# Rounding a float64 weight's high part before its low word is added, in a pooled attention and gated MLP kernel

## The chip, the cores and the metric

The kernel runs on one core of a Trainium2 chip. Its time is the device time of one launch in microseconds; times are medians over several runs. A profile records one further execution: its rows are in microseconds from the start of the span (first to last instruction). Engines are PE (TensorE, with PEld for its weight loads), DVE (VectorE), ACT (ScalarE), POOL (GpSimd) and SP, whose queue issues nearly all DMAs.

## The reference

For each of 8 batches, attention with 8 heads of 64 over 576 positions, with keys and values averaged over groups of 8 positions (72 pooled positions), then a gated MLP with a spatial gate:

```python
k_p = k.reshape(B, H, Sp, 8, D).mean(axis=3)          # v_p likewise
attn = softmax(scale * q @ k_p.T)                      # 576 x 72 per head
x = attn @ v_p                                         # (8, 576, 512)
h = gelu(x @ w_in)                                     # w_in (512, 1024)
u, v = h[..., :512], h[..., 512:]
v_n = (v - mean) / sqrt(var + 1e-6) * g_ln
v_s = einsum('ts,bsd->btd', w_sg, v_n) + b_sg
out = x + (u * v_s) @ w_out                            # w_out (512, 512)
```

`w_in` and `w_out` arrive as float64, all else as float32.

## The kernel before

All large products are made in three matmuls on numbers split in two: a value x is held as a high part, x rounded to the matmul's format (fp32r), and a low part, x minus the high part; high*high, high*low and low*high are accumulated. So each weight must become a pair of tiles: `wih`/`wil` for w_in, `woh`/`wol` for w_out.

**The float64 weights.** [...] The weights come in as six raw buffers of 1 MB (`load_w`: v0-1 and v2-3 for the v half of w_in, u0-1 and u2-3 for the u half, o0-1 and o2-3 for w_out), each holding two pieces of 128 x 512 numbers, low and high words alternating. `step_w` converts one of the twelve pieces in four steps:

1. ScalarE, L278: the high word is rescaled in exponent into a new tile `top` (tag y0 or y1).
2. DVE, L280: `top` is shifted left by 3. ScalarE, L281: the low word is turned, in its place, into the integer that its highest bits make.
3. POOL, L283: the two are added as integers into `top`, which now is the weight as float32. Then `move` (L221) rounds it into the high tile: on POOL (L223) for v0 to v3, u0, u3 and o2, on ScalarE (L225) for u1, u2, o0, o1 and o3.
4. `combine` (L227): `top` minus the high tile gives the low tile, on DVE for v3, u0, u2, o0 and o1, on POOL for the other seven.

**Buffers.** A tile takes a place in on-chip memory by its tag, and the next tile of that tag waits until every instruction that reads or writes the tile before it is done. The raw buffers borrow places that the batches need later: `load_w` gives v0-1 and v2-3 the tags `vhhi` and `vhlo`, u0-1 `ghi`, u2-3 `glo`, o0-1 `x32` (two places), and o2-3 `ghi` again, after u0-1. The gate of batch 0 (`ghi` for its high part, `glo` for its low part, made in `step_W`) takes the last two over.

**Order.** The order of all work is written out by hand (ORDER): each entry advances one step of one stage of one batch, and every engine issues its instructions in that order; semaphores are added by the framework. Stages are S (scores and softmax), T (attention turned round), V (attention times values), J and H (the v half), U (the u half), W (the spatial gate), O (the output product), Z (the store). Around o3, ORDER has: o3's third step, the first two steps of W0, W3 and W1, their third steps (the gate is rounded into `ghi`, on ScalarE in batch 0), o3's fourth step, then the fourth steps of W3 (on DVE, L228) and of W0 and W1 (on POOL, L228), then W2. The O stage reads `ghi` and `glo` by gate block d = 0, 1, 2, 3.

Of the kernel before, what the change touches and what calls it, by code (L numbers as in the profile page):

```python
# [8 lines left out]
F32 = mybir.dt.float32  # L9
# [5 lines left out]
ALU = mybir.AluOpType  # L15
# [79 lines left out]
def tile_pooled_attn_gmlp(ctx: ExitStack, tc: tile.TileContext, q, v0, vt0, k, v, vleft, w_in, w_sg, bg, w_out, out):  # L95
    nc = tc.nc
# [124 lines left out]
    def move(o, i, key):  # L221
        if key in OTHER:
            nc.gpsimd.tensor_copy(o, i)  # L223
        else:
            nc.scalar.copy(o, i)  # L225

    def combine(o, x, y, op, key):  # L227
        (nc.vector if key in OTHER else nc.gpsimd).tensor_tensor(o, x, y, op=op)  # L228
# [10 lines left out]
    def split(hi, lo, src, eng):  # L239
        nc.scalar.copy(hi, src)  # L240
        yield
        eng.tensor_tensor(lo, src, hi.bitcast(F32), op=ALU.subtract)
# [18 lines left out]
    def step_w(name, c):  # L261
        x = st["w", name, c // 2]
        n = x.shape[2] // 2
        x = x[:, c % 2:c % 2 + 1] if name == "v" else x[:, :, n * (c % 2):n * (c % 2 + 1)]
        hi, lo = {"v": (wih, wil), "u": (wih, wil), "o": (woh, wol)}[name]
        sl = (slice(None), slice(c, c + 1), slice(DF2, 2 * DF2)) if name == "v" else \
            (slice(None), slice(0, KC), slice(c * P, (c + 1) * P))
        hi, lo = hi[sl], lo[sl]
        if x.dtype == I32:

            rv = x.rearrange("p c (f w) -> p c f w", w=2)
            low, high = rv[:, :, :, 0], rv[:, :, :, 1]
            shape = [P, hi.shape[1], hi.shape[2]]
            top = per.tile(shape, I32, name="top", tag=f"y{c % 2}")
            nc.scalar.activation(top.bitcast(F32), high.bitcast(F32), AF.Prelu, scale=2.0 ** -112, alpha=2.0 ** 32)  # L278
            yield
            nc.vector.tensor_scalar(top, top, 3, None, op0=ALU.logical_shift_left)  # L280
            nc.scalar.activation(low, low.bitcast(U32), AF.Copy, scale=2.0 ** -29)  # L281
            yield
            nc.gpsimd.tensor_tensor(top, top, low, op=ALU.add)  # L283
            top = top.bitcast(F32)
            move(hi, top, f"{name}{c}h")
            yield
            combine(lo, top, hi.bitcast(F32), ALU.subtract, f"{name}{c}d")
            return
        yield from split(hi, lo, x, nc.gpsimd)

# [489 lines left out]
    def weight(name):  # L780
        if name[0] == "l":
            i = int(name[2])
            if name[1] == "s":
                load_wsg(i)
            else:
                load_w(name[1], i)
        else:
            if name not in going:
                going[name] = (step_s if name[0] == "s" else step_w)(name[0], int(name[1]))
            next(going[name], None)  # L790
# [70 lines left out]
```

## Time and profile before

| | |
|---|---|
| median of 3 runs | 498.75 us (498.43 to 500.1) |
| the profiled execution, own time | 500.95 us |
| its span | 499.2 us |
| PE busy | 492.0 us, 99% |
| DVE, ACT, POOL busy | 381.1, 271.4, 246.6 us |
| mean granted TensorE clock | 0.989 |

Busy time is counted by instruction; PE's overlaps its weight loads. In a timeline row, the first number is the start, the second the length, and the bracket at its end the idle time of that engine just before it, with what ended it. A row with "x2" merges two instructions that follow one another.

### The profile page before, as it was taken

What the parts mean: (1) busy time and instruction counts of PE and PEld (TensorE: products, weight loads), DVE (VectorE), ACT (ScalarE), POOL (GpSimd) and SP (SyncE); (2) the same over time, 40 slices, a digit from 0 to 9 for tenths busy, and PEclk for the clock granted to TensorE, in tenths of its full rate; (3) what the DMA queues carried; (4) which work ended last, traced back from release to release, by engine and by line L of the source; (5) the groups of instructions that cost most, each with busy time, mean ns of one, the idle gap of its engine ahead of it and who ended that gap; (6) DMA issues with size and microseconds to landing.
All of it is one profiled execution on the core that took longest, in us unless ns stands there. A gap on an engine that the chain in (4) does not pass through costs nothing.

```text
span 499.2 us, 9462 instructions
## 1 busy us (share of the span) xinstructions
PE 492.0 (99%) x3554; PEld 463.3 (93%) x3554; DVE 381.1 (76%) x593; ACT 271.4 (54%) x535; POOL 246.6 (49%) x330
## 2 busy tenths in 40 slices
PE   8989999999999999999999999999999999999997
PEld 8558999799899999999999999999999999999997
DVE  4967898677887887998889787978879757764462
ACT  4868984394747555658447364565735543314110
POOL 5875966544468357472484432845255720333010
PEclk9978999999999999999999999999999999999999
DMA  8992354666846352617434535143350333001003
GB/s 292 395 380 68 109 171 128 171 183 191 234 124 170 113 196 85 195 42 230 116 118 138 137 102 178 44 138 95 102 166 19 84 90 118 25 1 49 25 1 119
DMA packets 43034, 66.64 MB, mean 133 GB/s; under 512 B 5564, under 2 KB 22060, under 8 KB 42988
## 3 DMA queue, kind: packets, MB, share of 16 engines
q1 hardware_dynamic: 42700, 65.59, 43.5%
q8 instruction: 28, 0.46, 0.4%
q10 hardware_dynamic: 288, 0.44, 0.2%
q14 instruction: 18, 0.15, 0.1%
HBM read 47.14 MB, written 18.73 MB: 132 GB/s over the span
## 4 chain that ended last, share of the span: by engine, by line
PE 91%; DMA 4%; ACT 2%; DVE 2%; SPq 1%; issue 0%; ACTq 0%
PE mps L146 75%; PE aps L146 15%; DMA raw<-in_moe_w_in 3%; DMA out<-x 1%; PE aps L190 1%; SPq L237 1%; DVE ssum L466 0%; ACT e L457 0%; ACT x L219 0%; ACT L212 0%; ACT vg L480 0%; DVE x L755 0%; DVE x L217 0%; DVE ah L217 0%; DVE vl L424 0%
## 5 line engine op out<-in xcount | busy, mean ns | idle before, releaser
L146 PE MATMUL mps<-xhl,wih 128*128 128x288 f32 x512 | 84.2, 287 | 0.0
L146 PE MATMUL mps<-wih,xhl 128*128 128x512 f32 x256 | 79.4, 387 | 0.0
L146 PEld LDWEIGHTS mps<-xhl,wih 128*128 128x128 f32 x512 | 71.7, 189 | 0.3
L447 POOL TENSOR_TENSOR e<-e,ssum 128x720 f32<-128x720 f32 x29 | 41.9, 1444 | 60.3 <-DVE ssum L446 55.7
L146 PEld LDWEIGHTS mps<-wih,xhl 128*128 128x128 f32 x256 | 48.7, 191 | 6.8 <-DVE x L755 0.3
L146 PE MATMUL mps<-wsh,vhh 128*128 128x288 f32 x256 | 52.9, 288 | 0.0
L146 PE MATMUL mps<-wsh,vhl 128*128 128x288 f32 x256 | 52.3, 286 | 0.0
L146 PE MATMUL mps<-wsl,vhh 128*128 128x288 f32 x256 | 52.3, 286 | 0.0
L146 PE MATMUL mps<-xhl,wil 128*128 128x288 f32 x256 | 52.3, 286 | 0.0
L146 PE MATMUL mps<-ghi,woh 128*128 128x288 f32 x244 | 50.7, 288 | 0.0
L212 ACT ACT_TABLE_LOAD x39 | 50.0, 1283 | 0.6
L146 PE MATMUL mps<-ghi,wol 128*128 128x288 f32 x244 | 50.2, 286 | 0.0
L146 PE MATMUL mps<-glo,woh 128*128 128x288 f32 x244 | 50.2, 286 | 0.0
L470 POOL TENSOR_TENSOR rstd<-mv,eps 128x1 f32<-128x1 f32 (+1 forms) x40 | 11.8, 294 | 76.0 <-DVE mv L666 75.6
L146 PE MATMUL mps<-wil,xhl 128*128 128x512 f32 x128 | 47.2, 385 | 0.0
L234 POOL TENSOR_TENSOR xhl<-x,xhl 128x576 fp32r<-128x576 f32 x22 | 32.4, 1490 | 23.7 <-PE aps L146 12.0
L146 PE MATMUL aps<-kbd,qT 128*128 128x144 f32 x300 | 42.8, 293 | 0.0
L146 PEld LDWEIGHTS aps<-kbd,qT 128*128 128x128 f32 x300 | 40.2, 195 | 2.4 <-issue 0.9
L716 DVE SCALAR_TENSOR_TENSOR mps<-mps,both 128x576 f32<-128x576 f32 x32 | 26.1, 816 | 20.0 <-PE mps L146 20.0
L755 DVE TENSOR_TENSOR x<-mps,x 128x576 f32<-128x576 f32 x30 | 22.4, 750 | 24.4 <-PE mps L146 24.2
L146 PEld LDWEIGHTS mps<-wsh,vhh 128*128 128x128 f32 x256 | 40.0, 189 | 0.9 <-PE aps L146 0.4
L228 POOL TENSOR_TENSOR glo<-u,ghi 128x576 fp32r<-128x576 f32 x18 | 26.7, 1493 | 28.4 <-ACT ghi L219 18.1
(176 smaller groups left out, 1247.8 us busy)
## 6 DMA issues: line engine op xcount, KB each, us to landing
qT<-in_q SPq DMA_DIRECT2D x31, 288.0 KB, 4.2
out<-x SPq DMA_DIRECT2D x31, 288.0 KB, 2.6
kraw<-in_k SPq DMA_DIRECT2D x14, 576.0 KB, 4.5
vraw<-in_v SPq DMA_DIRECT2D x14, 512.0 KB, 5.0
al<-tfar SPq DMA_DIRECT2D x20, 288.0 KB, 3.4
tfar<-y SPq DMA_DIRECT2D x56, 80.0 KB, 1.9
raw<-in_moe_w_in SPq DMA_DIRECT2D x4, 1024.0 KB, 7.9
tfar<-y SPq DMA_DIRECT2D x56, 64.0 KB, 2.1
```

The costliest lines, as they stand in the source:

```text
L146: nc.tensor.matmul(o, lhsT, rhs, start=start, stop=stop)
L190: nc.tensor.transpose(ps[:rows, i * P:(i + 1) * P], src(i), ident if i < NT - 1 else swap)
L212: nc.scalar.activation(early, eps[:, 0:1], func)
L228: (nc.vector if key in OTHER else nc.gpsimd).tensor_tensor(o, x, y, op=op)
L234: nc.gpsimd.tensor_tensor(lo, x, hi, op=ALU.subtract)
L237: queue.dma_start(o, i)
L447: (nc.gpsimd if key in OTHER else nc.vector).tensor_tensor(e, e, rec.unsqueeze(3).broadcast_to([P, NT, 2, SP]), op=ALU.mult)
L470: nc.gpsimd.tensor_tensor(rstd, var, eps[:n, 1:2], op=ALU.add)
L716: nc.vector.scalar_tensor_tensor(vs, vs, gcol[:, d:d + 1], bbc.rearrange("p (a n) -> p a n", a=2), op0=ALU.mult, op1=ALU.add)
L755: nc.vector.tensor_tensor(x, seen(ps[:, :, 0:HALF]), x, op=ALU.add)
```

## The change

In the third step the rounding comes ahead of the addition and reads `top` as it is after the shift, without the low word's bits; it still goes to POOL or ScalarE by the same list. The sum is no longer written into `top` but over the low word in the raw buffer, at a step of two words, and the fourth step reads it there. The high part is so rounded from a number that lacks the low word; the low part is made from the full sum.

```diff
             yield
-            nc.gpsimd.tensor_tensor(top, top, low, op=ALU.add)
-            top = top.bitcast(F32)
-            move(hi, top, f"{name}{c}h")
-            yield
-            combine(lo, top, hi.bitcast(F32), ALU.subtract, f"{name}{c}d")
+            move(hi, top.bitcast(F32), f"{name}{c}h")
+            nc.gpsimd.tensor_tensor(low, top, low, op=ALU.add)
+            yield
+            combine(lo, low.bitcast(F32), hi.bitcast(F32), ALU.subtract, f"{name}{c}d")
             return
```

## Rows read from the trace of the kernel before

**Rows 1.** The page, engines: busy us, share of the span, instructions.
```profile
PE 492.0 (99%) x3554; PEld 463.3 (93%) x3554; DVE 381.1 (76%) x593; ACT 271.4 (54%) x535; POOL 246.6 (49%) x330
```

**Rows 2.** Waits of PE: us in total, times, longest.
```profile
PE aps L190 <- DVE xhl L232: 0.9, 1, 0.9
```

**Rows 3.** Windows: length, busy time of engines, granted clock, DMA share, GB/s.
```profile
30.00:45.00 15.00, 13.46 (x59) 10.16 (x58) 9.21 (x13) 9.35 (x33) 9.24 (x8) 0.66 0.71 240
80.00:85.00 5.00, 5.00 (x43) 5.00 (x42) 4.93 (x7) 0.67 (x1) 2.55 (x2) 1.00 0.73 185
```

**Rows 4.** Instructions of tile `top`: min/median/max ns, first and last start.
```profile
L283 POOL TENSOR_TENSOR top<-top,raw x12: 1286/1294/1628, 9.5 to 73.5; 128x512 int32<-128x512 int32 x12
...
L228 POOL TENSOR_TENSOR wol<-top,woh x2: 1286/1287/1288, 70.2 to 76.6; 128x512 fp32r<-128x512 f32 x2
```

**Rows 5.** Timeline, 73 to 84 us, around o3 and the gate of batch 0.
```profile
73.48 1.29 POOL L283 TENSOR_TENSOR top<-top,raw 128x512 int32<-128x512 int32 x1
...
74.81 0.62 ACT L225 CAST woh<-top 128x512 fp32r<-128x512 f32 x1 [1.58 <-POOL top L283]
...
76.14 1.88 ACT L219 CAST ghi<-u 128x576 fp32r<-128x576 f32 x3
...
76.60 1.29 POOL L228 TENSOR_TENSOR wol<-top,woh 128x512 fp32r<-128x512 f32 x1
...
77.66 0.84 DVE L228 TENSOR_TENSOR glo<-u,ghi 128x576 fp32r<-128x576 f32 x1
...
79.13 0.83 DVE L716 SCALAR_TENSOR_TENSOR mps<-mps,both 128x576 f32<-128x576 f32 x1 [0.63 <-PE mps L146]
...
80.78 0.67 ACT L219 CAST ghi<-u 128x576 fp32r<-128x576 f32 x1 [2.76 <-DVE u L719]
...
81.53 1.41 POOL L228 TENSOR_TENSOR glo<-u,ghi 128x576 fp32r<-128x576 f32 x1 [0.39 <-ACT ghi L219]
...
83.34 0.29 PE L146 MATMUL mps<-glo,woh 128*128 128x288 f32 x1
```

**Rows 6.** Timeline, 31 to 38 us, around u0, u1 and lo1.
```profile
31.77 0.38 SPq L237 DMA_DIRECT2D raw<-in_moe_w_out  x1
...
32.84 0.61 ACT L225 CAST wih<-top 128x512 fp32r<-128x512 f32 x1
...
33.54 1.27 POOL L228 TENSOR_TENSOR wil<-top,wih 128x512 fp32r<-128x512 f32 x1 [1.79 <-ACT wih L225]
...
34.39 0.96 DVE L228 TENSOR_TENSOR wil<-top,wih 128x512 fp32r<-128x512 f32 x1
...
37.86 0.33 SPq L237 DMA_DIRECT2D stail<-in_moe_w_sg  x1
```

**Rows 7.** Timeline, 49 to 69 us: what reads later.
```profile
49.27 1.39 PE L146 MATMUL aps<-kbd,qT 128*128 128x144 f32 x10
...
65.05 0.70 ACT L278 ACTIVATE top<-raw 128x512 f32<-128x512 f32 x1
...
66.82 0.69 DVE L683 TENSOR_TENSOR vht<-vg,vht 64x512 fp32r<-64x512 f32 x1
...
68.15 0.41 PE L146 MATMUL mps<-wth,vht 128*128 128x288 f32 x2
```

**Rows 8.** Waits of SP's queue, 0 to 100 us.
```profile
SPq L237 <- POOL top L283: 7.4, 1, 7.4
```

**Rows 9.** Timeline at 207.6 us: two remainders that meet.
```profile
207.71 1.41 POOL L228 TENSOR_TENSOR glo<-u,ghi 128x576 fp32r<-128x576 f32 x1
207.83 1.90 DVE L228 TENSOR_TENSOR glo<-u,ghi 128x576 fp32r<-128x576 f32 x1
```

**Rows 10.** Instructions of tile `glo`, as in rows 4.
```profile
L228 DVE TENSOR_TENSOR glo<-u,ghi x14: 707/758/1903, 77.7 to 482.4; 128x576 fp32r<-128x576 f32 x14
```

**Rows 11.** Timeline of PE's weight loads, 93 to 95 us.
```profile
93.58 0.19 PEld L146 LDWEIGHTS aps<-lt,vp 72*64 72x64 f32 x2 [0.33 <-ACT x L219]
94.24 0.13 PEld L146 LDWEIGHTS aps<-lt,vo 72*64 72x64 f32 x1 [0.47 <-DMA lt<-tfar]
```

## The prediction

> **What bounds the kernel now.** I read the page's engine line first, then PE's waits over the whole run, then the windows for the granted clock, and last the timeline of the stretches in which the twelve weight pieces are converted (7 to 78 us). PE is busy for 492.0 of 499.2 us [rows 1]. Its view of waits has seven rows that sum to 4.0 us, the last of them before 33 us; the longest in the stretch of the weights is the one of 0.9 us on DVE's L232 [rows 2], and no row of that view names the integer addition (L283), a weight's rounding (L223, L225) or its remainder (L228). So the conversion is not what PE waits for today. The reader is to see two consequences: making a high part earlier gives PE nothing by itself, and from 45 us on, where PE runs without a hole, every new stall on its path is paid in full. One more thing costs time early on: from 30 to 45 us the mean granted clock is 0.66, between the levels 1.2 and 2.4 GHz [rows 3], so (1 - 0.66) x 15 = 5.1 us of full-speed work are lost there, behind PE's pauses between 30 and 33 us.
>
> **The change part by part.** No instruction is added or removed: each of the twelve pieces keeps two ScalarE conversions, one shift, one integer addition, one rounding, one subtraction.
>
> *The rounding goes ahead of the addition.* It no longer waits for the addition, 1.29 us on POOL [rows 4]. Seven pieces round on POOL itself; there the two merely change places and the remainder comes at the same time. Five round on ScalarE, an engine in order, and only one of these was seen to wait: 1.58 us at 74.81, for o3 [rows 5]. What follows it on ScalarE within 0.8 us are two small scalings and then the roundings of the gate into `ghi` at 76.14, and those get a later bound below, so that wait is saved for nothing. For u1 the rounding stood at 32.84 behind ScalarE's own work, after the addition had been done for a microsecond (the addition's end let the transfer at 31.77 go), and POOL's subtraction at 33.54 still waits for it [rows 6]. Gain on PE's path: I take 0; the other end, a pause of PE that goes, is rival D.
>
> *The sum is written into the low word's place*, every second word, and read there by the subtraction. The addition already reads that place at stride two and takes 1.294 us at the median, against 1.287 for the subtraction with dense operands [rows 4]; no row writes with such a step on POOL. Bounds: 0 from that row, and a doubling, 1.29 us an instruction, as the far end. I take 0, the row it is nearest to. The five remainders on DVE read with the step too; the two latest of them stand in DVE's queue ahead of the tail's remainder, done at 66.82 + 0.69 = 67.51, which PE reads at 68.15 [rows 7]; 0.64 us is the cover, and beyond it PE would wait.
>
> The Trainium skill (GPSIMD Engine Reference, Performance pitfalls for Q7 kernels) says that a read step of more than 8 bytes costs half as much again per element; the step here is exactly 8 bytes, so by the page it costs nothing, as the addition's row bears out for the read. Past that step it would be about 0.65 us for each of the two instructions.
>
> *The raw buffer is held longer.* This is the part with a price. The last reader of a raw weight buffer was the addition; it is now the subtraction, one or two steps later. Whoever takes the buffer next waits for it: that this binds is seen at lo1, the second half of w_out, which goes into the buffer of u0 and u1 (tag `ghi`): SP sat 7.4 us on the addition [rows 8] and issued at 31.77. It will now wait for u1's subtraction (33.54 + 1.27 = 34.81) and u0's on DVE (34.39 + 0.96 = 35.35) [rows 6], so 35.37, 3.6 us later. Behind it in SP's queue stand the left-over values and one q tile, 36 to 37 us; the next issue after those waited till 37.86 for another reason and is not moved. The q tile's matmuls are at 49.27 and lo1's first reader at 65.05 [rows 7]: hidden, cost 0, unless lo1 landed over 20 us late.
>
> The second place is the gate. lo1's buffer, read by o2 and o3, passes to the `ghi` tile of batch 0. The additions were over at 73.48 + 1.29 = 74.77, so ScalarE's three roundings started at 76.14 without a wait. Now they wait for o3's subtraction, third in POOL's queue: 76.60 + 1.29 = 77.89 [rows 5]. Step by step:
> ghi0 starts at 77.93 (+1.79; 0.04 is what the rounding at 74.81 took after the addition's end at 74.77). Three took 1.88 us and one takes 0.67, so 0.60 lies between starts: ghi0 ends 78.60, ghi3 79.20, ghi1 79.80.
> POOL's remainder of d=0 starts at 78.65 and ends at 80.06. DVE's remainder of d=3, which began at 77.66 [rows 5], can start at 79.24 and then meets POOL's. What that costs is seen at 207 us: POOL's started 0.12 us ahead and kept its 1.41 us (to 209.12); DVE's took 1.90 (to 209.73), 0.61 after POOL's end [rows 9], against a median of 0.758 [rows 10]. So DVE is done at 80.67.
> DVE's next, L716 for d=2, began at 79.13 and now begins at 80.62, +1.49. By its own waits ScalarE's fourth rounding follows DVE's product, so 80.78 becomes 82.27, and POOL's remainder 81.53 becomes 82.99 and ends at 84.40.
> PE reads that remainder at 83.34 in step O1 [rows 5]; it was ready 0.40 us before. PE now stalls till 84.43: 1.09 us. (The fourth `ghi` itself, ready 82.94, costs 0.1 of the same stall.)
> Alone, without the meeting with POOL, the chain would be 0.67 shorter (80.00 instead of 80.67) and the stall 0.42; with ScalarE's wait hidden altogether it is 0. Above, the whole shift of 1.49 is the end.
>
> The Trainium skill (SBUF — State Buffer, Who interferes with whom) states that of a GpSimd read and a VectorE instruction with two SBUF inputs the second to issue is blocked until the first is done. The trace has the blocking, but DVE needs only 0.61 us after it; with a full 0.76 the stall would be 1.24 us.
>
> Does DVE's larger shift, 1.49 us, reach PE by another way? Through DVE, ScalarE evacuates the next batch's products late; at 93.58 PE waits on that evacuation, but at 94.24 on a transfer of attention rows [rows 11], 0.66 us later, that moves with PE's own progress. 1.49 - 1.09 = 0.40 is under 0.66. Nothing more.
>
> Sum: 0 + 0 + 0 + 1.09, about +1.1 us. Made against the profiled execution's own 500.95 us (span 499.2 and 1.75 around it), 502.05; that execution is 2.2 us above the median of the runs shown, 498.75, so there it is 499.85.
>
> **The rivals.** *A, the wait hides.* If o3's subtraction comes early, or DVE gets in ahead of POOL, the stall is 0 to 0.4 us: 498.75 to 499.15, say 499.0. For: the slack of 0.40 at 83.34. Against: the subtraction's row shows no idle time before it, so it can't come sooner.
> *B, the step of two costs on POOL: slower.* Place: o3's addition at 73.48 and its subtraction at 76.60, with no idle time of POOL before the second, so that each extra nanosecond moves the gate's rounding. With both doubled, +2.6 on top of 1.1; half of that is the likely size, 498.75 + 1.1 + 1.3 = 501.15. It decides from 0.4 us for both together, where the sum passes 1.5 us. For: no row of such a write. Against: the strided read costs 7 ns.
> *C, the stall drops the clock.* One such stretch lost 5.1 us; with the 1.1, about 505. For: the fall at 30 to 31 us followed pauses of under a microsecond. Against: around it PE is busy 5.00 of 5 us, at 1.00, where it was busy 13.46 of 15 from 30 to 45 [rows 3].
> *D, the early part shrinks: faster.* Roundings up to 1.3 us sooner shift POOL's normalisations, a pause of PE goes and the half-speed stretch shortens; up to -5.1, say -2.5 with the stall still paid: 497. Against: PE's waits name no weight instruction, and its pauses follow DVE copies and ScalarE copies that the change leaves in place.
>
> **How the numbers follow.** Forecast 0.55 (499.85; by itself 499.1 to 500.3), A 0.16, B 0.14, C 0.04, D 0.11. A measurement of this kernel tells about 0.3%, 1.5 us, from no change: 497.25 to 500.25. Above it lie C, 0.13 of B and 0.11 of the forecast, if the stall is 1.5 or more: 0.28. Below it D: 0.11. The rest, 0.61, is within. For 8 in 10 the range leaves out D's far part and the upper ends of B and C: 498.2 to 501.5.
>
> **What would show it.** ScalarE's first `ghi` rounding idle until POOL's o3 subtraction ends, near 77.9; DVE's remainder of d=3 long, 1.4 us or more; PE idle about 1 us near 83 to 84.5, a wait on POOL's L228; lo1's issue near 35.4 with nothing of PE moved by it; the addition and subtraction on POOL still about 1.29. The prediction is wrong if `ghi` starts at 76.1, if POOL's addition takes over 1.5 us, or if the granted clock from 30 to 45 us differs from 0.66.

## The result: slower by 1.4%, and the profile after

| | before | after |
|---|---|---|
| median, first comparison (4 runs each) | 499.43 us | 505.33 us (504.13 to 507.52) |
| ratio, first comparison | | 1.0137, 95% interval 1.0092 to 1.0182 |
| ratio, second comparison (6 runs of after, 23 of before) | | 1.0103, 1.0064 to 1.0143 |
| profiled execution, own time / span | 500.95 / 499.2 us | 506.53 / 504.8 us |

The change makes the kernel 5 to 7 us slower (the medians of the two comparisons lie 5.9 and 5.5 us apart). The forecast was 499.85 with a range up to 501.5: wrong. The spread inside one kernel goes with the granted clock: in one comparison the kernel before took 497.2 us at a mean clock of 1.00 and 502.7 at 0.99. The loss itself is mostly not the clock: in the second comparison, at the same mean clock of 0.997, after took 503.0 to 503.6 us (three runs) and before 498.3 to 498.9 (five); at 0.993, 504.6 to 505.7 (three) and 499.7 to 501.0 (two).

PE does the same work in a span that is 5.6 us longer. First the page's engine line of after (busy us, share, instructions; against [rows 1]), then the longest rows of its PE waits (us in total, times, longest; of the two that are not new, L199 waits for a constant at the start and L232 is [rows 2]).

```profile
PE 494.1 (98%) x3554; PEld 464.9 (92%) x3554; DVE 384.5 (76%) x593; ACT 271.2 (54%) x535; POOL 248.0 (49%) x330
```

```profile
PE aps L146 <- ACT top L278: 2.2, 1, 2.2
PE aps L146 <- POOL ident masks.py:199: 1.4, 1, 1.4
PE mps L146 <- ACT vg L660: 0.9, 1, 0.9
PE aps L190 <- DVE xhl L232: 0.7, 1, 0.7
PE mps L146 <- POOL glo L228: 0.7, 1, 0.7
```

Three waits are new: 2.2, 0.9 and 0.7 us. Only the last was forecast. In time order:

**The wait of 2.2 us, at 21 to 24 us.** Timeline of the kernel before, then of after (start, length, engine, line; in brackets the idle time before). `ssum<-ssum,eps` is a tiny addition on DVE, 128 x 10 numbers, in batch 0's softmax. L440 of before is L439 of after; the integer addition is L283 of before, L284 of after.

```profile
13.28 1.29 POOL L283 TENSOR_TENSOR top<-top,raw 128x512 int32<-128x512 int32 x1 [0.43 <-DVE top L280]
13.99 0.62 DVE L440 TENSOR_TENSOR ssum<-ssum,eps 128x10 f32<-128x10 f32 x1
...
16.47 0.16 DVE L440 TENSOR_TENSOR ssum<-ssum,eps 128x10 f32<-128x10 f32 x1
16.55 1.39 POOL L447 TENSOR_TENSOR e<-e,ssum 128x720 f32<-128x720 f32 x1
...
19.78 0.61 POOL L223 CAST wih<-top 128x512 fp32r<-128x512 f32 x1
20.33 0.17 DVE L440 TENSOR_TENSOR ssum<-ssum,eps 128x10 f32<-128x10 f32 x1
20.47 1.28 POOL L228 TENSOR_TENSOR wil<-top,wih 128x512 fp32r<-128x512 f32 x1
20.67 0.69 DVE L217 COPY lt<-aps 72x576 f32<-72x576 f32 x1
...
21.46 1.47 PE L146 MATMUL aps<-kbd,qT 128*128 128x144 f32 x10
```

```profile
13.82 1.30 POOL L284 TENSOR_TENSOR raw<-top,raw 128x512 int32<-128x512 int32 x1
14.03 1.11 DVE L439 TENSOR_TENSOR ssum<-ssum,eps 128x10 f32<-128x10 f32 x1
...
16.45 1.40 POOL L446 TENSOR_TENSOR e<-e,ssum 128x720 f32<-128x720 f32 x1
17.02 0.85 DVE L439 TENSOR_TENSOR ssum<-ssum,eps 128x10 f32<-128x10 f32 x1
...
20.04 1.30 POOL L284 TENSOR_TENSOR raw<-top,raw 128x512 int32<-128x512 int32 x1
20.58 0.89 DVE L465 TENSOR_REDUCE ssum<-e 128x10 f32<-128x720 f32 x1
21.42 1.30 POOL L228 TENSOR_TENSOR wil<-raw,wih 128x512 fp32r<-128x512 f32 x1
21.51 1.24 DVE L439 TENSOR_TENSOR ssum<-ssum,eps 128x10 f32<-128x10 f32 x1
...
22.91 0.69 DVE L217 COPY lt<-aps 72x576 f32<-72x576 f32 x1
...
23.70 1.68 PE L146 MATMUL aps<-kbd,qT 128*128 128x144 f32 x7 [2.19 <-ACT top L278]
```

Read the ends. After: 14.03 + 1.11 = 15.14, and POOL's addition ends at 15.12; 17.87 against 17.85; 21.51 + 1.24 = 22.75 against 22.72. Each of these DVE additions starts behind a two-operand instruction of POOL and ends only with it. Only the first of the three meets the integer addition, which runs 0.54 us later because the rounding now goes first (13.82 for 13.28). The other two follow from the first: DVE, about 0.5 us late, comes behind POOL's normalisation (17.02 against 16.45), where it had been 0.08 ahead (16.47 against 16.55), and then, 1.2 us late, behind the remainder (21.51 against 21.42), where it had been 0.14 ahead (20.33 against 20.47). Before, the three took 0.62 + 0.16 + 0.17 = 0.95 us, now 3.20: 2.25 more. DVE's copy `lt` moves from 20.67 to 22.91, 2.24, and PE's matmul from 21.46 to 23.70, 2.24. In both kernels PE starts 0.10 after the copy's end; the row names ScalarE's L278, but the copy's end is what it follows (the matmul writes the place that the copy reads): the distance is 0.10 to 0.11 in 13 of the 14 traces of this case, and 0.24 in the other (after_noeps).

**The clock.** Windows of before and after (length, busy of PE, PEld, DVE, ACT, POOL, granted clock, DMA share, GB/s; 30 to 45 of before is in [rows 3]):

```profile
20.00:30.00 10.00, 9.58 (x64) 6.43 (x62) 8.94 (x17) 8.51 (x17) 8.20 (x8) 1.00 1.05 392
```

```profile
20.00:30.00 10.00, 7.81 (x41) 6.21 (x40) 8.11 (x13) 5.24 (x12) 8.03 (x8) 0.83 1.05 391
30.00:45.00 15.00, 13.29 (x62) 8.77 (x61) 9.47 (x15) 9.21 (x18) 7.99 (x6) 0.66 0.58 201
```

From 30 to 45 us the mean clock is 0.66, as before (part of that time at 1.2 in place of 2.4 GHz), and behind PE's 2.2 us of idleness a second such stretch has come: (1.00 - 0.83) x 10 = 1.7 us of full-speed work. PE's score product at 37.71 in before is at 41.36, 3.65 late (u1's subtraction, 33.54 in [rows 6], is at 37.25): 2.24 of the wait and 1.41 of the clock. In the seven traces with this early wait (1.2 to 2.3 us) the clock of 20 to 30 us is 0.66 or 0.83, in the seven without it 1.00. But the stretch behind it, from 30 to 45 us, can then be missing (after_again, below), so 1.41 is the figure of this execution, and no run isolates the clock's share.

**The wait of 0.9 us, at 59 us.** u2's remainder, in before and in after:

```profile
48.56 0.63 DVE L228 TENSOR_TENSOR wil<-top,wih 128x512 fp32r<-128x512 f32 x1
48.81 1.63 POOL L447 TENSOR_TENSOR e<-e,ssum 128x720 f32<-128x720 f32 x1 [1.02 <-DVE ssum L446]
```

```profile
52.35 1.39 POOL L446 TENSOR_TENSOR e<-e,ssum 128x720 f32<-128x720 f32 x1 [0.99 <-DVE ssum L445]
52.45 1.83 DVE L228 TENSOR_TENSOR wil<-raw,wih 128x512 fp32r<-128x512 f32 x1 [0.28 <-issue]
...
59.30 0.48 PE L146 MATMUL mps<-wih,xta 128*128 128x512 f32 x1 [0.94 <-ACT vg L660]
```

Before, DVE began 0.25 ahead of POOL; now it idles 0.28 ("issue"), comes 0.10 behind, and takes 1.83 for 0.63. The batch statistics behind it in DVE's queue are late, and through them ScalarE and PE.

**The gate, at 81 to 89 us,** against [rows 5]:

```profile
81.33 1.31 POOL L228 TENSOR_TENSOR wol<-raw,woh 128x512 fp32r<-128x512 f32 x1
...
82.67 1.82 ACT L219 CAST ghi<-u 128x576 fp32r<-128x576 f32 x3 [1.81 <-POOL wol L228]
...
83.42 3.30 POOL L228 TENSOR_TENSOR glo<-u,ghi 128x576 fp32r<-128x576 f32 x2 [0.78 <-ACT ghi L219]
83.95 1.50 DVE L228 TENSOR_TENSOR glo<-u,ghi 128x576 fp32r<-128x576 f32 x1 [1.47 <-ACT ghi L219]
...
87.01 0.67 ACT L219 CAST ghi<-u 128x576 fp32r<-128x576 f32 x1 [2.52 <-DVE u L718]
...
87.76 1.40 POOL L228 TENSOR_TENSOR glo<-u,ghi 128x576 fp32r<-128x576 f32 x1 [1.04 <-ACT ghi L219]
...
89.22 0.51 PE L146 MATMUL mps<-glo,woh 128*128 128x288 f32 x2 [0.72 <-POOL glo L228]
```

PE's matmul at 68.15 in [rows 7] is now at 72.89, 4.74 late; the one at 83.34 in [rows 5] is at 89.22, 5.88 late. The gate costs 5.88 - 4.74 = 1.14.

So, along PE's path in this execution: 2.24 (DVE's tiny additions) + 1.41 (the clock behind them) + 0.94 (u2) + 0.15 (not traced) + 1.14 (the gate) = 5.88 at 89 us, and 5.6 at the end of the span.

### The profile page after: what moved, and what is told of

Same layout as the page of the kernel before. It is cut to its first block, busy times and chain, and to the rows that moved or that the text cites. A ratio compares the mean times of both kernels' runs of the same rounds, so it can differ in the third digit from the quotient of the medians.

```text
span 504.8 us, 9460 instructions
## 1 busy us (share of the span) xinstructions
PE 494.1 (98%) x3554; PEld 464.9 (92%) x3554; DVE 384.5 (76%) x593; ACT 271.2 (54%) x535; POOL 248.0 (49%) x330
## 4 chain that ended last, share of the span: by engine, by line
PE 83%; DVE 9%; ACT 3%; DMA 2%; issue 1%; POOL 1%; SPq 0%; ACTq 0%; POOLq 0%
PE mps L146 69%; PE aps L146 14%; DMA raw<-in_moe_w_in 1%; DVE ssum L465 1%; DVE nmax L494 1%; DVE kp L356 1%; DVE e L451 1%; PE aps L190 0%; ACT top L278 0%; DVE ssum L439 0%; DVE vp L356 0%; ACT ghi L219 0%; DMA tfar<-y 0%; DVE wil L228 0%; DVE top L280 0%
```

## The experiments

Three theories. *Order* (the expectations call it the port theory): the rounding ahead of the addition moves POOL's two-operand instructions onto DVE's tiny additions. *Buffer*: the sum in the raw buffer holds the buffer and delays its readers (the gate, u2). *Step*: writing every second word costs on POOL. A kernel with more lines has other line numbers beyond the change. Four of the kernels stand against 35 runs of before, four against 28, four against 23. Behind a name stand the ratio, its 95% interval and the us that the ratio makes of 498.5; the differences of the medians are between 0.2 us smaller and 0.9 larger.

**v_new and uo_new: the new form for one half of the weights alone.**

```diff
-            move(hi, ...); addition into low; yield; combine(lo, low, ...)
+            if name == "v":          # uo_new: name != "v"
+                move(hi, ...); addition into low; yield; combine(lo, low, ...); return
+            ...                      # else the form of before
```

> Only the four v pieces are converted in the new form, the u and o pieces in the old one. Port theory: what the trace of after shows at 14 to 24 us is VectorE's tiny softmax-sum additions (two operands in on-chip memory) shut out behind POOL's integer additions, which the new order has moved onto them; so this kernel alone brings the late copy at 22.9 us, PE's wait of about 2.2 us at 23.7 and the clock loss behind it: about 3.6 us, 503 us. Buffer theory (the raw buffers held longer cause the loss): v's buffers are taken over late, so nothing: 499.4. Step theory (writing and reading every second word is slow): four of twelve pieces, about 2 us: 501.4.

> The eight u and o pieces in the new form, the v pieces in the old one. Port theory with the buffer as a smaller part: the first 24 us are as before, and what is left is PE's wait of 0.9 us near 59 (u2's remainder on VectorE starting behind a POOL normalisation) and of 0.7 us at the gate: 1.5 to 2.5 us, about 501.4. Buffer theory: all of it, 505. Step theory: eight of twelve pieces, about 4 us: 503.4.

v_new: 1.0068 (1.0046 to 1.009), +3.4 us, with tiny additions of 1.10, 0.85 and 1.22 us and PE's wait of 2.0 on L278. uo_new: 1.0028 (1.0007 to 1.0049), +1.4, tiny additions of 0.61, 0.16 and 0.17 as before, and the 0.7 on the gate's remainder; u2's wait of 0.9, expected too, is not there. The early loss belongs to the four v pieces; u and o carry about what the prediction gave the whole change, +1.1.

**after_noeps and before_noeps: DVE's tiny additions of batch 0 left out** (so 1e-9 is missing in those denominators), in after and in before.

```diff
+        if b == 0 and key in OTHER:
+            return
         if key in OTHER:
             nc.vector.tensor_tensor(ssum, ssum, eps[:, 0:1]..., op=ALU.add)
```

> The changed kernel, and in batch 0 the four additions of 1e-9 to the softmax sums are left out (the reciprocal reads the sums as they are). Port theory: VectorE has no tiny two-operand instruction left to be shut out at 14, 17 and 21.5 us, so PE's wait at 23.7 us shrinks from 2.2 to under 0.5 us, and the kernel is 3 to 4 us faster than the changed one: about 502 us. Buffer and step theories: four instructions of 0.17 us less, no change: 505.

> The kernel before with the same four additions left out, as the yardstick for the run on the changed one. Only one of them was long before (0.62 us at 14.0), and the stretch behind it waits for a transfer that lands at 17.0 us. All theories: within 1 us of before, 498.5 to 500.

after_noeps: 1.0011 (0.9993 to 1.0028); before_noeps: 1.0 (0.9979 to 1.0021). Four instructions of 0.16 to 0.6 us are worth nothing in before and 4.6 to 6.3 us in after: the largest part of the loss hangs on them, more than the 3 to 4 us expected. The wait of 2.2 is gone, u2's 0.9 with it, and the granted clock of its trace is 1.00 from 20 to 45 us; the gate's 0.7 is still there. The reciprocal that now comes first is not held: it began at 14.02, inside POOL's addition of 13.81, and took 0.22.

**order_pool: the new order alone, where POOL rounds.** The sum stays in `top`.

```diff
+            first = f"{name}{c}h" in OTHER      # rounded on POOL
+            if first: move(hi, top, ...)
+            nc.gpsimd.tensor_tensor(top, top, low, op=ALU.add)
+            if not first: move(hi, top, ...)
```

> The new order (rounding ahead of the addition) only for the seven pieces whose rounding is on POOL; the sum stays in top, so the raw buffer is released by the addition as before. If the loss comes from the order alone (POOL's addition now lies beside DVE's tiny additions of batch 0): those take about 1.1, 0.85 and 1.2 us as in the changed kernel, PE has one wait of about 2 us near 21 to 24 us, no wait on the gate's remainder, and the time is that of the run that changed the v pieces alone, +2.5 to +5 us. If the place of the sum, written at a step of two words, makes the loss: none of this, and +0 to +0.5 us.

1.0032 (1.0007 to 1.0058), +1.6 us: less than expected. The first two tiny additions took 1.22 and 0.82, the third 0.17. Its timeline:

```profile
20.34 1.28 POOL L286 TENSOR_TENSOR top<-top,raw 128x512 int32<-128x512 int32 x1
...
21.68 0.17 DVE L444 TENSOR_TENSOR ssum<-ssum,eps 128x10 f32<-128x10 f32 x1
21.70 1.29 POOL L228 TENSOR_TENSOR wil<-top,wih 128x512 fp32r<-128x512 f32 x1
...
22.02 0.69 DVE L217 COPY lt<-aps 72x576 f32<-72x576 f32 x1
...
22.81 2.54 PE L146 MATMUL aps<-kbd,qT 128*128 128x144 f32 x10 [1.24 <-ACT raw L281]
```

DVE starts 0.02 us ahead of POOL and goes free; in after it starts 0.09 behind and pays 1.24. The copy is at 22.02, PE 0.10 behind its end, and PE's wait 1.2 in place of 2.2. POOL comes later here because the addition overwrites what the rounding reads: it began 0.69 after the rounding began, 0.57 in after. So the order alone, with the sum left in `top`, brings the first two delays; the third was a matter of a tenth of a microsecond, and without it the loss stays below the +2.5 expected.

**place: the new place alone.** Old order, the sum in the raw buffer.

```diff
-            move(hi, top.bitcast(F32), f"{name}{c}h")
             nc.gpsimd.tensor_tensor(low, top, low, op=ALU.add)
+            move(hi, low.bitcast(F32), f"{name}{c}h")
```

> The old order (addition, rounding, remainder), but the sum goes into the low word's place in the raw buffer for all twelve pieces. If order alone makes the early loss: the tiny additions of batch 0 as in the kernel before (0.6, 0.2, 0.2 us), no wait of 2 us near 21 to 24 us, only the gate's wait of 0.7 us that a raw buffer held longer makes, +0.7 to +1.5 us in all. If the step of two words costs on POOL or in the roundings that now read it too: additions or roundings on POOL over 1.4 us and +3 us or more.

1.0053 (1.0031 to 1.0076), +2.6 us: more than the 0.7 to 1.5 expected. Early nothing is lost (tiny additions 0.61, 0.22, 0.17; no wait of 2 us), and POOL's additions take 1.29, so the step is not it. PE has the 0.7 on the gate, and the 0.9 on L660 as well: u2's remainder starts at 47.36, 0.09 behind POOL, and takes 1.85. About half a us is left; its trace has one more wait of PE, 0.6 on ScalarE's L370 at 11 us, that place_o23 (below) lacks, so it may belong to this execution alone.

**o23_old: after, with the old form for o2 and o3**, whose buffer passes to the gate.

```diff
+            if (name, c // 2) != ("o", 1):
                 ...                  # new form; o2 and o3: old
```

> The changed kernel with the old form for the two pieces o2 and o3 alone, whose raw buffer passes to the gate's high part: it is released by the addition again. PE's wait of 0.7 us on the gate's remainder near 83 us goes and nothing else, the early loss and the half-clock stretch stay: 0.5 to 1 us less than the changed kernel, so +5 to +6.3 us. If the gate's wait were the seed of the loss, the time would come back to within 1.5 us of before.

1.0081 (1.005 to 1.0112), +4.0 us, less than the +5 to +6.3 expected; the gate's wait is gone, those of 2.1 and 0.9 are there. Against after's own 1.0137 and 1.0103 that is 1.1 to 2.8 us; the intervals overlap, so the 1.1 of the trace is not contradicted and no more. The gate is not the seed.

**after_eps1: the tiny additions with a constant** in place of the second operand.

```diff
-            nc.vector.tensor_tensor(ssum, ssum, eps[:, 0:1]..., op=ALU.add)
+            nc.vector.tensor_scalar(ssum, ssum, 1e-9, None, op0=ALU.add)
```

> The changed kernel, with the tiny additions of batch 0 on DVE written as an addition of a constant, so that they read one operand in on-chip memory in place of two; their place in the order and their result stay. If they were held up because they read two operands beside POOL's addition: 0.1 to 0.2 us each again, no wait of 2 us near 21 to 24 us, time as with these additions left out, +0.5 to +1.5 us. If any small DVE instruction there is held up, or the order of the queues does it: 0.9 to 1.2 us each as in the changed kernel, +5 to +7 us.

1.0095 (1.0061 to 1.0128): nothing gained; my expectation was wrong. They took 1.10, 0.85 and 1.23:

```profile
21.73 1.29 POOL L228 TENSOR_TENSOR wil<-raw,wih 128x512 fp32r<-128x512 f32 x1
21.83 1.23 DVE L439 TENSOR_SCALAR ssum<-ssum 128x10 f32<-128x10 f32 x1
```

One operand is no protection for an addition of a constant. But it is not any small instruction that is held. The reduction in after at 20.58 took 0.89 beside POOL's addition of 20.04, and all 27 of its line take 0.85 to 0.90. The reciprocal was free in after_noeps, and so is, in after, an addition of a constant that writes to PSUM (`aps`, where the matmuls write) in place of SBUF, the memory of the other tiles:

```profile
78.22 1.30 POOL L284 TENSOR_TENSOR raw<-top,raw 128x512 int32<-128x512 int32 x1
78.54 0.16 DVE L436 TENSOR_SCALAR aps<-ssum 128x10 f32<-128x10 f32 x1
```

The Trainium skill (SBUF — State Buffer, SBUF: two separate sides) says that the lock concerns a DVE instruction with two SBUF inputs, and also one in a mode that uses both ports; VectorE: DVE Perf Modes (What auto-detection actually checks) gives such a mode, once it is enabled for the instruction, to one with a single source whose source and destination lie in SBUF, with outermost lengths that are even or equal. Both fit these rows, the addition into PSUM among them; that the held addition ran in that mode no row shows.

**after_again: after once more.**

> The changed kernel once more, unaltered, for more runs and a second trace. If its loss sits where the first trace showed it: the wait of 2.2 us near 21 to 24 us, DVE's tiny additions of 1.1, 0.85 and 1.2 us, the wait of 0.9 us on ScalarE's L660 near 59 us and of 0.7 us on the gate's remainder all come back; the time is 502.5 to 506 us against 498.3, the spread being the length of the half-clock stretch. If any of the three waits is an accident of one execution, it is missing in this trace.

1.0103 (1.0064 to 1.0143), 504.1 us. All three waits are back (2.1, 0.9, 0.7), the tiny additions took 1.10, 0.85 and 1.23. What differs is the clock: 0.66 from 20 to 30 us, then 1.00 from 30 to 45, where the first trace had 0.83 and 0.66.

**order_act: the new order alone, where ScalarE rounds.** As order_pool, with `not in OTHER`.

> The new order only for the five pieces that ScalarE rounds (u1, u2, o0, o1, o3); the sum stays in top. If the loss comes from POOL's additions beside DVE's tiny additions, from the later u2 remainder and from the longer held buffer: none of the three is touched, and the time is 0 to +0.5 us, with no new wait of PE. If rounding from the shifted word ahead of the sum costs or gains by itself (ScalarE's wait of 1.58 us for o3 goes): over 0.7 us either way.

1.0126 (1.0084 to 1.0168), +6.3 us: wrong. I had forgotten that here the addition overwrites the tile that the rounding still reads, so that POOL now waits for ScalarE. From its timeline, and its PE waits:

```profile
61.09 2.55 POOL L286 TENSOR_TENSOR top<-top,raw 128x512 int32<-128x512 int32 x2 [3.18 <-ACT woh L225]
62.43 1.76 DVE L228 TENSOR_TENSOR wol<-top,woh 128x512 fp32r<-128x512 f32 x1 [1.32 <-POOL top L286]
```

```profile
PE mps L146 <- ACT u L706: 2.2, 1, 2.2
PE mps L146 <- ACT vg L665: 1.6, 1, 1.6
```

So the run doesn't test what it was made for. It shows what the change's second place buys: with the sum elsewhere, POOL doesn't wait for ScalarE's rounding.

**u2_old: after, with the old form for u2 alone.**

```diff
+            if (name, c) != ("u", 2):
                 ...                  # new form; u2: old
```

> The changed kernel with the old form for u2 alone, whose remainder DVE then reads from the dense top. If the sum in the raw buffer makes DVE start that remainder late, behind POOL's normalisation: DVE takes about 0.63 us there in place of 1.83, PE's wait of 0.9 us on ScalarE's L660 is gone, the waits of 2.2 and 0.7 us stay, and the time is 0.9 to 1.3 us below that of the changed kernel in the same call. If the late start is an accident of the earlier shift: the 0.9 us stays or comes up elsewhere, and the time is that of the changed kernel.

1.0076 (1.0049 to 1.0102) against 1.0103 for after in the same comparison, so 1.3 us less by the ratios and 1.5 by the medians, though the intervals overlap. The trace is plain: PE's wait of 0.9 is gone, those of 2.1 and 0.7 stay, and DVE is ahead of POOL again:

```profile
51.40 0.63 DVE L228 TENSOR_TENSOR wil<-top,wih 128x512 fp32r<-128x512 f32 x1
51.66 1.63 POOL L453 TENSOR_TENSOR e<-e,ssum 128x720 f32<-128x720 f32 x1 [1.02 <-DVE ssum L452]
```

**place_o23: place, with o2 and o3 in `top`.**

```diff
+            held = low if (name, c // 2) != ("o", 1) else top
             nc.gpsimd.tensor_tensor(held, top, low, op=ALU.add)
```

> The old order for all pieces, the sum in the raw buffer for all but o2 and o3, whose buffer is so released by the addition. Against the run with the sum in the raw buffer for all twelve (+2.6 us): PE's wait of 0.7 us on the gate's remainder is gone, that of 0.9 us near 54 us stays; +1 to +2 us. If the sum's place costs on every piece: still +2 us or more.

1.0038 (1.0009 to 1.0066), +1.9 us: the gate's 0.7 gone, u2's 0.9 there. As expected, within intervals that overlap.

No version was faster than the kernel before.

## Why the prediction was wrong

*The rounding goes ahead of the addition: the failed step.* It says "there the two merely change places and the remainder comes at the same time", and takes 0 for it. The remainder does (15.33 before, 15.20 after). But the addition now runs 0.54 us later, and DVE's tiny addition, which ends only with it, met its last 0.58 us before (13.99 to 14.57) and meets 1.09 of it now (14.03 to 15.12). That delay put the next two behind a normalisation and a remainder of POOL. In place of 0, the term cost 2.24 us of PE's path in the profiled execution, and 1.41 more at half clock behind it. v_new and after_noeps show it: the v pieces carry +3.4 us, and without those additions after is back at +0.5. (Whether a rounding holds DVE too, no row shows: the nearest, the addition at 20.33 beside the rounding of 19.78, overlaps it by 0.06 us.) The working had the contention itself, with a price, from the rows at 207 us [rows 9], and used it at the gate only. And it argued that PE's waits name no weight instruction; they could not, because the chain passes through DVE's copy `lt`, whose end PE followed by 0.10 us already in before.

*The step of two: right.* POOL's addition in after, and the two strided remainders, by tile (min/median/max ns, first and last start; against [rows 4]):

```profile
L284 POOL TENSOR_TENSOR raw<-top,raw x12: 1288/1297/1475, 9.7 to 78.2; 128x512 int32<-128x512 int32 x12
...
L228 POOL TENSOR_TENSOR wol<-raw,woh x2: 1306/1310/1315, 74.8 to 81.3; 128x512 fp32r<-128x512 f32 x2
```

3 ns for the write, 23 for the read. Rival B falls.

*lo1: right.* It waits for u0's subtraction on DVE and issues 3.6 + 3.7 (the early shift) later than the 31.77 of [rows 6]; PE has no wait for it.

```profile
38.04 1.06 DVE L228 TENSOR_TENSOR wil<-raw,wih 128x512 fp32r<-128x512 f32 x1
39.16 0.38 SPq L237 DMA_DIRECT2D raw<-in_moe_w_out  x1
```

*The gate: right, and in size.* Shift the prediction's times by the 4.73 by which o3's subtraction came late (76.60 to 81.33): `ghi` 77.93 becomes 82.66 (82.67 measured), DVE's remainder 79.24 becomes 83.97 (83.95, 1.50 long, 1.43 forecast), the fourth `ghi` 82.27 becomes 87.00 (87.01). The stall was 1.14 for 1.09, of which one row of the waits shows 0.72.

*u2: not seen; it cost 0.94.* The cost of DVE's five remainders was looked for in their length (DVE's read at a step cost 0.71 against 0.63 where it was not held), not in their start. Why DVE idles 0.26 to 0.29 us ahead of u2's is open: in after a semaphore instruction of DVE stands ahead of it (0.05 us at 52.0) that before has not, but uo_new and after_noeps have the same one, and there it started without that idle time (46.37 and 45.06) and kept 0.72 and 0.71. The price is shown (u2_old), the cause of the late start is not.

*Rival C had the right companion at the wrong place.* A second half-clock stretch came behind a stall, the early one of 2.2 us; the gate's brought none (1.00 from 78 to 90). The "granted clock from 30 to 45 us" was named as a sign, and stayed at 0.66 in the first trace while the loss was at 20 to 30; in the second it was 1.00, so that the sign tells little of this change.

## What to carry to other kernels

When two instructions of one engine change places, ask for each not only who reads its result but whom it shuts out while it runs: list the short DVE instructions beside both positions, the old and the new. A wait view that names none of the moved instructions clears them only if the instruction that PE waits for, and the one ahead of it in its queue, have slack. Where a result is kept in another buffer, look at both sides: who gets the buffer later, and whether its reader still starts ahead of its neighbour on the other engine (u2's did not).

## What the runs showed of the hardware

A DVE addition of 128 x 10 numbers within SBUF took 0.16 to 0.22 us when it began 0.02 to 0.15 us ahead of POOL's two-operand instruction, and up to 1.24 when it began 0.09 behind: a tenth of a microsecond in order decided over one in time. A reciprocal, a reduction, and an addition that writes to PSUM ran beside such an instruction at their usual 0.22, 0.89 and 0.16 us. POOL, when second, lost less: its normalisation took 1.63 for 1.39 behind a DVE remainder of 0.63. The half-clock stretch between 20 and 45 us is not a property of the program alone: after had 0.83 and 0.66 in one execution, 0.66 and 1.00 in another.
